# Attention scores with tokens on the partitions: exponentials with row sums, shares turned by DMA, and a listed step order, in a fused attention and gated feed-forward kernel

## The chip, the cores and the metric

The kernel runs on one NeuronCore of a Trainium2 chip. The metric is the device time of one execution in microseconds (us); lower is better. The time before is 1031.74 us, the median of 3 runs (1031.52 to 1032.04).

A core has five engines that run side by side, each through its own instructions in order, and that wait for one another by semaphores: TensorE (PE, matrix products; PEld is its weight load), VectorE (DVE), ScalarE (ACT), GpSimd (POOL) and SyncE (SP), which here only issues DMAs. SBUF is the working memory of 128 partitions; PSUM is the memory of eight banks that TensorE writes to (a bank holds 512 fp32 for each partition).

## The reference

Four images, each with 12288 tokens and a map that is pooled to 768 keys; the keys are also the values. Softmax attention is followed by a gated feed-forward layer.

```python
B, C, Hh, Ww = (4, 128, 384, 32)            # q: (4, 12288, 128), kv: (4, 384, 32, 128)
kv_pool = kv.reshape(B, H // r, r, W // r, r, C).mean(axis=(2, 4))    # r = 4
kv_flat = kv_pool.reshape(B, -1, C) @ w_sr
k = v = kv_flat                             # 768 keys of 128
s = scale * (q @ k.transpose(0, 2, 1))
s = s - s.max(-1, keepdims=True)
a = np.exp(s)
a /= a.sum(-1, keepdims=True) + 1e-09
x = (a @ v).reshape(B * S, D)               # 49152 tokens of 128
gate = np.maximum(x @ w_gate, 0.0)          # 128 x 1536
val = x @ w_val                             # 128 x 1536
out = gate * val @ w_out                    # 1536 x 128
```

## The kernel before

The tokens are worked through in 96 tiles of T = 512, 24 for each image. The 768 keys are six chunks of 128 (`NJC`), the 1536 inner features twelve blocks of 128 (`NFB`). The first four tiles' attention and some of the feed-forward layer are in an opening of its own, a list of words (`OPENING`, lines 69 to 79). From then on a loop over k (line 610) runs over the tiles, and within it a loop over twelve steps (line 621). Each k works on several tiles at once: the scores of tile k, the values of tile k-1, the feed-forward projections of tile k-3 (`LAG` = 3), the output projection of tile k-4. The order of the program is the order on each engine (`manual_schedule`): no scheduler moves anything.

One step issues:

- `out_proj` (line 398): one matmul of 512 columns into the tile's output bank.
- `value_proj` (line 372): one matmul of 512 columns; ScalarE copies it as fp16 to `val` (line 378).
- on even steps `scores` (line 290): one chunk of 128 keys is stationary and the 512 tokens move, so keys lie on the partitions of the bank; ScalarE's exponential (line 295) writes fp16 to `aT`.
- on odd steps `values` (line 297), twice: `aT` is stationary, 128 tokens at a time, and the values of one chunk move, 128 columns and a column of ones that gives the sum of the exponentials. 24 such matmuls make a tile. When half of the tokens are done, VectorE takes the reciprocal of the sums (`keep_sums`, line 313) and multiplies (`keep_values`, line 321) into `x16`; after the second half a DMA transpose of four blocks of 128x128 (`x_turn`, line 329) turns `x16` to `xT`, with features on the partitions, as the projections need it.
- `gate_proj` (line 381): one matmul of 512 columns, then VectorE's `hT = max(gate, 0) * val` (line 388).

After the last step VectorE turns the output bank in 32x32 blocks (`out_turn`, line 415), GpSimd scales it (line 423), and in the next tile four stores go out from SP (line 634).

Ahead of each of the images 1 to 3, in the last 12 or so tiles of the image before, the next keys are made: loads of `kv` by SP (line 184), additions of pixels by GpSimd (`pool_pixels`, lines 190 to 202, one run for each of six tiles), a transpose by VectorE and DMAs (`turn_blocks`, line 265), a projection (`project`, line 257), and a DMA transpose to values (line 284). The queries come in groups of four tiles: GpSimd issues the loads (line 114), SP a transpose of 16 blocks (line 124).

All eight PSUM banks are one pool that is handed out in turn (`bank`, line 87). SP issues the DMAs of its queue in the order of the program.

Of the kernel before, what the change touches and what calls it, by code (L numbers as in the profile page):

```python
# [16 lines left out]
def kernel(  # L17
# [41 lines left out]
    LEAD = GRP  # L59
    qk_scale = 1.0 / math.sqrt(C)  # L60
# [18 lines left out]
    """.split()  # L79
    SUMS = [{}, {}, {}, {"a": [0, 1], "b": ["s", 2]}, {"a": [0, 1], "b": ["s", 2], "c": ["s", 3]}, {"a": [0, 1]}]  # L80
# [4 lines left out]
    psum = ctx.enter_context(tc.tile_pool(name="psum", bufs=8, space=bass.MemoryType.PSUM))  # L85

    def bank(shape, dtype=FP32):
        return psum.tile(shape, dtype, tag="bank", name="bank_ps")
# [38 lines left out]
    def q_load_pair(i):  # L127
        q32 = work.tile([128, 2, NS, C], FP32, tag="q32", bufs=2, name="q32")
        nc.sync.dma_start(  # L129
            q32, q[0, i * T : (i + 2) * T, :].rearrange("(p i s) c -> p i s c", i=2, s=NS)  # L130
        )
        for n in range(2):
            q32s[i + n] = q32[:, n]
# [24 lines left out]
    def q_turned(i):  # L158
        copy_on(f"qT{i}", qTs[0][:, i * NS : (i + 1) * NS, :], q_banks.pop(i))
# [16 lines left out]
    def kv_load(b, pair, lines=range(r), queues=(nc.sync,)):  # L176
        if (b, pair) not in kv_in:
            kv_in[b, pair] = work.tile([128, r, 2, r, C], FP32, tag="kv_in", bufs=3, name="kv_in")
# [4 lines left out]
        for dh in lines:  # L183
            queues[dh % len(queues)].dma_start(  # L184
                parts[:, dh].rearrange("p h dw c -> p (h dw c)"), rows[dh]
            )
# [3 lines left out]
    def pool_pixels(eng, b, pair, h):  # L190
        parts = kv_in[b, pair]
        s2 = work.tile([128, 2, r, C], FP32, tag="kv_s2", bufs=1)
        for i in range(2):
            eng.tensor_tensor(s2[:, i], parts[:, 2 * i, h], parts[:, 2 * i + 1, h], op=ALU.add)  # L194
# [9 lines left out]
    def line(chunk, dh):  # L204
        return kv_in[0, chunk // 2][:, dh, chunk % 2]
# [26 lines left out]
    def turned(name, chunk):  # L232
        kvT = work.tile([128, 128], FP32, tag="kvT_chunk", bufs=3, name="kvT_chunk")
        copy_on(name, kvT, kv_Ts[chunk])
# [8 lines left out]
    def keep_keys(name, jc):  # L243
        pr, engine = key_ps.pop(jc), engine_of(name)
# [9 lines left out]
    def keep_chunk_values(name, jc):  # L254
        copy_on(name, kv16[:, 0, jc, C : 2 * C], value_ps.pop(jc))

    def project(b, pair):
        pr = bank([128, 4, 2, 32])
        nc.tensor.matmul(pr, w_sr_f32, kv_Ts.pop((b, pair)), start=True, stop=True)  # L259
        nc.vector.tensor_scalar(  # L260
            kv16[:, b, 2 * pair : 2 * pair + 2, 0:C].rearrange("c h (i p) -> c h i p", p=32),
            pr.rearrange("c i h p -> c h i p"), 1.0 / (r * r), None, op0=ALU.mult,
        )

    def turn_blocks(b, pair):

        blocks = work.tile([128, 4, 2, 32], FP32, tag="kv_blocks", bufs=2)
# [22 lines left out]
    def scores(k, jc):  # L290
        if k not in aTs:
            aTs[k] = work.tile([128, NJC, T], FP16, tag="aT", bufs=5, name="aT")
        s_ps = bank([128, T])
        nc.tensor.matmul(s_ps, kv16[:, k // NST, jc, 0:C], qT_of(k), start=True, stop=True)  # L294
        nc.scalar.activation(aTs[k][:, jc, :], s_ps, AF.Exp, scale=qk_scale)  # L295

    def values(k, jc, half):
        if jc == 0:
            x_banks[k, half] = bank([128, 2, C + 1])
            if half == 0:  # L300
                x16s[k] = work.tile([128, NS, C], FP16, tag="x16", bufs=3, name="x16")
        x_ps = x_banks[k, half]
        for i in range(2):
            s = 2 * half + i
            nc.tensor.matmul(  # L305
                x_ps[:, i, :], aTs[k][:, jc, s * 128 : (s + 1) * 128],
                kv16[:, k // NST, jc, C : 2 * C + 1],
                start=(jc == 0 and i == 0), stop=(jc == NJC - 1), skip_group_check=True,
            )

    def keep_sums(k, half):
        rinvs[k, half] = work.tile([128, 2, 1], FP32, tag="rinv", bufs=4, name="rinv")
        nc.vector.reciprocal(rinvs[k, half], x_banks[k, half][:, :, C : C + 1])  # L313

    def keep_values(k, half, engine=nc.vector):
        x_ps, rinv = x_banks.pop((k, half)), rinvs.pop((k, half))
        if engine is nc.scalar:
            for i in range(2):
                nc.scalar.mul(x16s[k][:, 2 * half + i, :], x_ps[:, i, 0:C], rinv[:, i])
        else:  # L320
            nc.vector.tensor_tensor(  # L321
                x16s[k][:, 2 * half : 2 * half + 2, :], x_ps[:, :, 0:C],
                rinv.to_broadcast([128, 2, C]), op=ALU.mult,
            )

    def x_turn(k):
        x16 = x16s.pop(k)
        xT = work.tile([128, NS, 128], FP16, tag="xT", bufs=5, name="xT")
        nc.sync.dma_start_transpose(xT, x16.rearrange("p s c -> p (s c)"))
        xTs[k] = xT.rearrange("c s p -> c (s p)")  # L330

# [12 lines left out]
    def lead_kept(name, k):  # L344
        xTs[k] = work.tile([128, NS, 128], FP16, tag="xT", bufs=5, name="xT").rearrange("c s p -> c (s p)")
        copy_on(name, xTs[k], x_banks.pop(k))
# [12 lines left out]
    def lead_scales():  # L359
        turned = work.tile([128, NS * 4, 32], FP32, tag="o_sb", bufs=3, name="sums_turned")  # L360
        nc.vector.transpose(turned.rearrange("p x m -> p (x m)"), x_banks.pop("sums"))
# [9 lines left out]

    def value_proj(k, fb):
        va_ps = bank([128, T])
        nc.tensor.matmul(  # L374
            va_ps, wv16[:, fb * 128 : (fb + 1) * 128], xTs[k], start=True, stop=True
        )
        val = work.tile([128, T], FP16, tag="val", bufs=6, name="val")
        nc.scalar.copy(val, va_ps)  # L378
        vals[k, fb] = val

    def gate_proj(k, fb):
        if k not in hTs:
            hTs[k] = work.tile([128, NFB, T], FP16, tag="hT", bufs=3, name="hT")
        g_ps = bank([128, T])
        nc.tensor.matmul(  # L385
# [313 lines left out]
```

## Time and profile before

| | us |
|---|---|
| median of 3 runs | 1031.74 |
| the profiled execution | 1031.77 |
| its span, from the first instruction to the last | 1029.7 |
| from one tile's DMA transpose of `x16` to the next | 10.42 |

The profile is of one execution. Busy time is time in which an engine worked on an instruction; TensorE's matmuls are pipelined, so that one of 512 columns lasts 380 ns while the next one starts 216 ns after it. In the lists of groups each line has: line of the code, engine, operation, what is written and what is read, shapes, count, then the busy time in us, the mean ns of one, and the engine's idle time just ahead of them with what ended it. The answer by stretches of time has, for each stretch: its length, busy us of PE, PEld, DVE, ACT and POOL (with the number of instructions), the granted clock of TensorE as a fraction, the mean busy share of the 16 DMA engines, and GB/s. A timeline has: start in us, length in us, engine (SPq is SP issuing a DMA), line, operation, names and shapes. The DMA issues of a steady stretch show what SP does in a tile:

```profile
498.48 1.22 SPq L329 DMA_TRANSPOSE xT<-x  x1
499.79 2.59 SPq L634 DMA_DIRECT2D out_dram<-o_sb  x4
508.90 1.21 SPq L329 DMA_TRANSPOSE xT<-x  x1
510.30 3.90 SPq L124 DMA_TRANSPOSE qT<-q  x1
514.28 2.60 SPq L634 DMA_DIRECT2D out_dram<-o_sb  x4
519.33 1.21 SPq L329 DMA_TRANSPOSE xT<-x  x1
```

### The profile page before, as it was taken

What the parts mean: (1) busy time and instruction counts of PE and PEld (TensorE: products, weight loads), DVE (VectorE), ACT (ScalarE), POOL (GpSimd) and SP (SyncE); (2) the same over time, 40 slices, a digit from 0 to 9 for tenths busy, and PEclk for the clock granted to TensorE, in tenths of its full rate; (3) what the DMA queues carried; (4) which work ended last, traced back from release to release, by engine and by line L of the source; (5) the groups of instructions that cost most, each with busy time, mean ns of one, the idle gap of its engine ahead of it and who ended that gap; (6) DMA issues with size and microseconds to landing.
All of it is one profiled execution on the core that took longest, in us unless ns stands there. A gap on an engine that the chain in (4) does not pass through costs nothing.

```text
span 1029.7 us, 19928 instructions
## 1 busy us (share of the span) xinstructions
PE 1023.3 (99%) x6521; PEld 541.8 (53%) x6521; DVE 908.1 (88%) x1663; ACT 909.3 (88%) x1745; POOL 284.5 (28%) x308
## 2 busy tenths in 40 slices
PE   8999999999999999999999999999999999999998
PEld 5455555555555555555555555555555555555555
DVE  3889899998989898998889898989898898989898
ACT  5988899888889888888988889988888988888987
POOL 2502156511211124742112121664121221111110
PEclk9999999999999999999999999999999999999999
DMA  9836386352553648826346167573552434613122
GB/s 321 113 53 83 88 192 148 72 95 39 88 62 55 75 122 160 169 55 88 56 63 88 32 86 154 133 168 58 84 75 45 73 54 66 87 32 65 34 42 52
DMA packets 327807, 93.33 MB, mean 91 GB/s; under 512 B 307480, under 2 KB 320664, under 8 KB 327704
## 3 DMA queue, kind: packets, MB, share of 16 engines
q1 hardware_dynamic: 312584, 77.97, 37.8%
q0 software_dynamic: 14688, 12.98, 11.0%
q8 instruction: 51, 0.84, 0.3%
q10 hardware_dynamic: 432, 1.11, 0.3%
q14 instruction: 52, 0.43, 0.1%
HBM read 53.94 MB, written 26.35 MB: 78 GB/s over the span
## 4 chain that ended last, share of the span: by engine, by line
PE 97%; DMA 2%; SPq 0%; issue 0%; ACT 0%; ACTq 0%
PE bank_ps L374 24%; PE bank_ps L385 24%; PE bank_ps L407 23%; PE bank_ps L305 12%; PE bank_ps L294 12%; DMA kv_in<-in_kv_dram 1%; PE bank_ps L393 1%; DMA q<-in_q_dram 1%; PE bank_ps L259 0%; PE bank_ps L339 0%; PE bank_ps L353 0%; SPq L184 0%; PE bank_ps L227 0%; SPq L502 0%; PE bank_ps L241 0%; SPq L129 0%
## 5 line engine op out<-in xcount | busy, mean ns | idle before, releaser
L388 DVE SCALAR_TENSOR_TENSOR hT<-bank_ps,val 128x512 f16<-128x512 f32 x1152 | 757.2, 686 | 91.0 <-ACT val L378 70.6
L378 ACT CAST val<-bank_ps 128x512 f16<-128x512 f32 x1152 | 677.6, 590 | 103.0 <-PE bank_ps L374 100.8
L374 PE MATMUL bank_ps<-xT,wv 128*128 128x512 f16 x1152 | 436.9, 380 | 0.0
L385 PE MATMUL bank_ps<-xT,wg 128*128 128x512 f16 x1152 | 436.6, 379 | 0.0
L407 PE MATMUL bank_ps<-hT,wo 128*128 128x512 f16 x1116 | 423.5, 380 | 0.0
L295 ACT ACTIVATE aT<-bank_ps 128x512 f16<-128x512 f32 x576 | 345.7, 604 | 0.6 <-PE bank_ps L294 0.6
L423 POOL TENSOR_SCALAR o_sb<-o_t 128x512 f32<-128x512 f32 x89 | 132.4, 1487 | 664.8 <-DVE rinv L313 646.8
L305 PEld LDWEIGHTS <-aT 128*128 128x128 f16 x2208 | 170.6, 98 | 130.3
L294 PE MATMUL bank_ps<-qT,kv 128*128 128x512 f16 x576 | 217.5, 379 | 0.0
L305 PE MATMUL bank_ps<-kv,aT 128*128 128x129 f16 x2208 | 215.5, 221 | 0.0
L374 PEld LDWEIGHTS <-wv 128*128 128x128 f16 x1152 | 112.6, 98 | 133.2 <-issue 0.7
L385 PEld LDWEIGHTS <-wg 128*128 128x128 f16 x1152 | 112.7, 98 | 68.2 <-DMA wg<-in_moe_w_gate_dram 0.3
L407 PEld LDWEIGHTS <-wo 128*128 128x128 f16 x1116 | 109.1, 98 | 66.1 <-DMA wo<-in_moe_w_out_dram 0.4
L294 PEld LDWEIGHTS <-kv 128*128 128x128 f16 x576 | 56.3, 98 | 67.1 <-DVE kv L248 0.4
L321 DVE TENSOR_TENSOR x<-bank_ps,rinv 128x256 f16<-128x256 f32 x184 | 78.1, 425 | 6.4
L415 DVE STREAM_TRANSPOSE o_t<-bank_ps 128x512 f32<-128x512 f32 x93 | 65.7, 706 | 0.0
L114 POOL DMA_DIRECT2D q<-in_q_dram x84 | 46.0, 553 | 0.3 <-ACT val L378 0.3
L194 POOL TENSOR_TENSOR s<-kv_in 128x512 f32<-128x512 f32 x36 | 44.8, 1265 | 0.0
L313 DVE RECIPROCAL rinv<-bank_ps 128x2 f32<-128x2 f32 x184 | 26.8, 146 | 0.0
L196 POOL TENSOR_TENSOR s<-s 128x512 f32<-128x512 f32 x18 | 22.8, 1265 | 1.4
L198 POOL TENSOR_TENSOR c<-s 128x256 f32<-128x256 f32 x18 | 13.0, 725 | 1.4
L393 PEld LDWEIGHTS <-hT 128*128 128x128 f16 x144 | 10.1, 98 | 5.8
(66 smaller groups left out, 121.1 us busy)
## 6 DMA issues: line engine op xcount, KB each, us to landing
kv_in<-in_kv_dram SPq DMA_DIRECT2D x46, 512.0 KB, 7.3
out_dram<-o_sb SPq DMA_DIRECT2D x353, 64.0 KB, 2.2
q<-in_q_dram POOLq DMA_DIRECT2D x84, 128.0 KB, 4.7
xT<-x SPq DMA_TRANSPOSE x92, 2.4
out_dram<-o_sb SPq DMA_DIRECT2D x80, 16.0 KB, 1.5
placed<-blocks SPq DMA_DIRECT2D x9, 128.0 KB, 1.9
kvT<-placed SPq DMA_DIRECT2D x36, 32.0 KB, 1.9
kv_in<-in_kv_dram ACTq DMA_DIRECT2D x2, 512.0 KB, 7.2
```

The lines of the kernel that those rows point to most:

```text
L114: nc.gpsimd.dma_start(q16[32 * j : 32 * (j + 1)].rearrange("t (i s) c -> t i s c", i=GRP), rows[j])
L294: nc.tensor.matmul(s_ps, kv16[:, k // NST, jc, 0:C], qT_of(k), start=True, stop=True)
L295: nc.scalar.activation(aTs[k][:, jc, :], s_ps, AF.Exp, scale=qk_scale)
L305: nc.tensor.matmul(x_ps[:, i, :], aTs[k][:, jc, s * 128 : (s + 1) * 128], kv16[:, k // NST, jc, C : 2 * C + 1], start=(jc == 0 and i == 0) ...
L321: nc.vector.tensor_tensor(x16s[k][:, 2 * half : 2 * half + 2, :], x_ps[:, :, 0:C], rinv.to_broadcast([128, 2, C]), op=ALU.mult,)
L374: nc.tensor.matmul(va_ps, wv16[:, fb * 128 : (fb + 1) * 128], xTs[k], start=True, stop=True)
L378: nc.scalar.copy(val, va_ps)
L385: nc.tensor.matmul(g_ps, wg16[:, fb * 128 : (fb + 1) * 128], xTs[k], start=True, stop=True)
L388: nc.vector.scalar_tensor_tensor(hTs[k][:, fb, :], g_ps, 0.0, vals.pop((k, fb)), op0=ALU.max, op1=ALU.mult)
L407: nc.tensor.matmul(o_banks[k], wo16[:, fb, :], hTs[k][:, fb, :], start=fb == 0, stop=fb == NFB - 1)
L415: nc.vector.transpose(o_t, o_banks.pop(k))
L423: nc.gpsimd.tensor_scalar(to, o_by, 1.0 / X_SCALE**2, None, op0=ALU.mult)
```

## The change

From the fifth tile on (those of the loop) the scores are made with the tokens on the partitions. `score_block` (the word s) takes 128 tokens as stationary and moves all 768 keys, as 512 and 256 columns, into a tile of two banks, of which there is one. `exp_block` (e) is one exponential of 768 elements, which also writes the sum of each token's exponentials. A tile later `invert` (r) takes the reciprocals of the sums, `share` (n) multiplies the fp16 exponentials in place by reciprocal and scale, and each of the four blocks is turned by a DMA transpose of six 128x128 blocks (`a_turn`). Another tile later `values` (x) has the values stationary and the 512 tokens moving, six matmuls, and the result is `xT` at once: `keep_values` (kA) is a plain copy by VectorE, and `keep_sums`, `x16` and `x_turn` are gone.

PSUM is now six single banks, taken from a list in the order in which the program frees them, and the tile of two banks; the opening has all eight until its last eight words. Products and what drains them are now issued apart (v and y, g and h, `project` and `keep_projected`), in the order of a list `STEADY`, the same for each tile. Two of the four stores of an output move from SP to GpSimd. The loads of the next image go out one line at a time, three steps apart, into two buffers instead of three; a few buffers of the opening share memory with later ones.

```diff
+    LAST = [f"{head}{n}" for n in range(NFB) for head in "ovygh"] + ["oT"]
+    STEADY = """
+        s0 g6 o0 e0 v6 y6 v10 r o1 v9 tb s1 y10 h6 o2 n3 g7 o3 v7 o4 y9 v8 v1 y7 o5 o6
+        g1 n0 g9 y1 o7 e1 n1 n2 o8 h7 v0 g10 o9 h9 o10 y0 y8 v3 h1 v2 h10 o11 y3 oT s2
+        g0 h0 e2 g2 g8 h8 x0 y2 h2 x2 v11 x5 s3 g11 x4 y11 x3 v5 e3 x1 y5 h11 v4 y4 P g4
+        kA pk g5 h5 g3 h4 h3
+    """.split()
...
     def bank(shape, dtype=FP32):
-        return psum.tile(shape, dtype, tag="bank", name="bank_ps")
+        n = next(n for n in free_banks if n < usable[0])
+        free_banks.remove(n)
+        ps = pools[n // 6].tile(shape, dtype, tag=f"bank{n}", bufs=1, name="bank_ps")
+        bank_numbers[id(ps)] = n, ps
+        return ps
...
+    def score_block(k, s):
+        b = k // NST
+        if s == 0:
+            a16s[k] = work.tile([128, NS, J], FP16, tag="a16", bufs=4, name="a16")
+            a_sums[k] = work.tile([128, NS], FP32, tag="a_sums", bufs=2, name="a_sums")
+        s_ps = s_banks[s] = wide.tile([128, 1024], FP32, tag="wide", name="wide_ps")
+        qT = qTs[k // GRP][:, k % GRP * NS + s, :]
+        for j0, j1 in ((0, 4), (4, NJC)):
             nc.tensor.matmul(
-                x_ps[:, i, :], aTs[k][:, jc, s * 128 : (s + 1) * 128],
-                kv16[:, k // NST, jc, C : 2 * C + 1],
-                start=(jc == 0 and i == 0), stop=(jc == NJC - 1), skip_group_check=True,
+                s_ps[:, j0 * 128 : j1 * 128], qT, kv16[:, b, j0:j1, 0:C], start=True, stop=True
             )
...
+    def exp_block(k, s):
+        nc.scalar.activation(
+            a16s[k][:, s, :], s_banks.pop(s)[:, 0:J], AF.Exp, scale=qk_scale, accum_out=a_sums[k][:, s : s + 1]
+        )
+
+    def invert(k):
+        inverse = work.tile([128, NS], FP32, tag="inverse", bufs=2, name="inverse")
+        nc.vector.reciprocal(inverse, a_sums[k])
+        a_sums[k] = inverse
+        aTs[k] = work.tile([128, NJC, T], FP16, tag="aT", bufs=AT_BUFS, name="aT")
+
+    def share(k, s):
+        nc.vector.tensor_scalar(
+            a16s[k][:, s, :], a16s[k][:, s, :], a_sums[k][:, s : s + 1], X_SCALE,
+            op0=ALU.mult, op1=ALU.mult,
+        )
+
+    def a_turn(k, s0, s1):
+        aT = aTs[k].rearrange("k j t -> k (j t)").rearrange("k (x p) -> k x p", p=128)
+        nc.sync.dma_start_transpose(
+            aT[:, s0 * NJC : s1 * NJC], a16s[k][:, s0:s1, :].rearrange("p s j -> p (s j)")
+        )
+
+    def values(k, jc):
+        first = k not in x_banks
+        if first:
+            x_banks[k], x_left[k] = bank([128, T]), NJC
+        x_left[k] -= 1
+        aT = aTs[k].rearrange("k j t -> k (j t)").rearrange("k (s j p) -> k j s p", s=NS, j=NJC)
+        nc.tensor.matmul(
+            x_banks[k], kv16[:, k // NST, jc, C : 2 * C], aT[:, jc],
+            start=first, stop=x_left[k] == 0,
+        )
+
+    def keep_values(k):
+        xT = work.tile([128, NS, 128], FP16, tag="xT", bufs=4, name="xT")
         xTs[k] = xT.rearrange("c s p -> c (s p)")
+        nc.vector.tensor_copy(xTs[k], freed(x_banks.pop(k)))
...
+    for at, word in enumerate(OPENING):
+        usable[0] = 8 if at < len(OPENING) - 8 else 6
         open_step(word)
...
+    opening.close()
+    wide = ctx.enter_context(tc.tile_pool(name="psum_wide", bufs=1, space=bass.MemoryType.PSUM))
...
+    def image_step(k, b, at, step):
+        if step % 3 == 1 and 0 <= at < NJC and at % 2 == 0:
+            kv_load(b, at // 2, [step // 3])
+        if step == 3 and 0 <= at - 2 < NJC:
+            pool_pixels(nc.gpsimd, b, (at - 2) // 2, at % 2)
+        pair, odd = divmod(at - 4, 2)
+        if 0 <= pair < NJC // 2:
+            if moves and step > 4:
+                nc.sync.dma_start(*moves.pop())
...
+        kO, kF, kV = k - LAG - 1, k - LAG, k - 2
+        for word in STEADY if k < last else LAST:
+            head, n = word.rstrip("0123456789"), int(word.lstrip("abcdefghijklmnopqrstuvwxyzADPT") or 0)
+            if head == "o":
+                out_proj(kO, n)
+                for queue in (nc.gpsimd, nc.sync):
+                    if out_moves and n >= 2:
+                        queue.dma_start(*out_moves.pop())
+                if b < B:
+                    image_step(k, b, at, n)
...
+            elif head in ("v", "y", "g", "h"):
+                if kF < NT:
+                    {"v": value_proj, "y": keep_value, "g": gate_proj, "h": gated}[head](kF, n)
+            elif head in ("s", "e"):
+                if k < NT:
+                    {"s": score_block, "e": exp_block}[head](k, n)
+            elif head in ("r", "n"):
+                if LEAD <= k - 1 < NT:
+                    if head == "r":
+                        invert(k - 1)
+                    else:
+                        share(k - 1, n)
+                        a_turn(k - 1, n, n + 1)
...
+            elif LEAD <= kV < NT:
+                if head == "x":
+                    values(kV, n)
+                else:
+                    keep_values(kV)
```

The words o, v, g are the matmuls of the output, value and gate projections, y and h what drains v and g, oT the turning of the outputs, tb, P and pk the steps of the next image's keys.

## The prediction

> **What bounds the kernel now.** I read the busy shares first, then the same shares by stage, the chain of waits, the groups of instructions and last the timeline of one tile. The busy shares alone name three candidates (TensorE 99%, VectorE and ScalarE 88%). The stages decide: TensorE is busy through every microsecond of three long stretches.
>
> ```profile
> PE 1023.3 (99%) x6521; PEld 541.8 (53%) x6521; DVE 908.1 (88%) x1663; ACT 909.3 (88%) x1745; POOL 284.5 (28%) x308
> ```
>
> ```profile
> 60.00:340.00 280.00, 280.00 (x1771) 147.25 (x1769) 251.66 (x460) 250.97 (x482) 80.15 (x80) 1.00 0.49 87
> 340.00:620.00 280.00, 280.00 (x1771) 147.26 (x1770) 251.91 (x463) 251.08 (x482) 84.57 (x85) 1.00 0.54 91
> 620.00:900.00 280.00, 280.00 (x1774) 147.43 (x1773) 251.85 (x461) 251.11 (x482) 82.99 (x82) 1.00 0.51 91
> ```
>
> The chain that ended last is TensorE too, and the answer to the chain query gives each line's share to a tenth:
>
> ```profile
> by line: PE bank_ps L374 24.2%; PE bank_ps L385 24.1%; PE bank_ps L407 23.4%; PE bank_ps L305 12.2%; PE bank_ps L294 11.8%; DMA kv_in<-in_kv_dram 1.1%; PE bank_ps L393 0.8%; DMA q<-in_q_dram 0.8%; PE bank_ps L259 0.4%; PE bank_ps L339 0.3%;
> ```
>
> So a saving on TensorE counts in full, as long as the other engines still deliver inside a tile. A tile is 10.42 us (the tokens' transposes start at 498.48, 508.90, 519.33). VectorE is busy 251.7 of 280 us, 9.37 us of a tile: it has only 1 us to give. The groups that the change touches, then 1.6 us of VectorE's and GpSimd's timelines:
>
> ```profile
> L388 DVE SCALAR_TENSOR_TENSOR hT<-bank_ps,val 128x512 f16<-128x512 f32 x1152 | 757.2, 686 | 91.0 <-ACT val L378 70.6
> L378 ACT CAST val<-bank_ps 128x512 f16<-128x512 f32 x1152 | 677.6, 590 | 103.0 <-PE bank_ps L374 100.8
> L295 ACT ACTIVATE aT<-bank_ps 128x512 f16<-128x512 f32 x576 | 345.7, 604 | 0.6 <-PE bank_ps L294 0.6
> L423 POOL TENSOR_SCALAR o_sb<-o_t 128x512 f32<-128x512 f32 x89 | 132.4, 1487 | 664.8 <-DVE rinv L313 646.8
> L305 PE MATMUL bank_ps<-kv,aT 128*128 128x129 f16 x2208 | 215.5, 221 | 0.0
> L321 DVE TENSOR_TENSOR x<-bank_ps,rinv 128x256 f16<-128x256 f32 x184 | 78.1, 425 | 6.4
> L415 DVE STREAM_TRANSPOSE o_t<-bank_ps 128x512 f32<-128x512 f32 x93 | 65.7, 706 | 0.0
> ```
>
> ```profile
> 655.81 2.49 POOL L194 TENSOR_TENSOR s<-kv_in 128x512 f32<-128x512 f32 x2
> 658.38 1.27 POOL L196 TENSOR_TENSOR s<-s 128x512 f32<-128x512 f32 x1
> 659.73 0.72 POOL L198 TENSOR_TENSOR c<-s 128x256 f32<-128x256 f32 x1
> 660.53 0.45 POOL L202 TENSOR_TENSOR kv_s<-c 128x128 f32<-128x128 f32 x1
> ```
>
> In the groups, the mean of one is its latency; back to back the engines overlap. Four L388 at 508.75 take 2.47 us, 0.617 each; ScalarE starts at 499.44, 499.92 and 500.41, so 0.49 each. In the last fence, GpSimd pools the next image's pixels in one run of 5.2 us. That happens in 18 tiles (L194 x36, two for each), six ahead of each new image.
>
> **What the Trainium skill says.** "VectorE: DVE Perf Modes", the perf-mode tier table: a tensor_scalar on 16-bit data in SBUF runs at four elements a cycle, 693 ns for 2048. The trace has no such row; its nearest, the opening's 128x512 casts from SBUF at L98 (422 ns, against 692 from PSUM), does show an SBUF source going faster. "SBUF — State Buffer", Who interferes with whom: such an instruction takes a port pair that VectorE shares with GpSimd; the pair is an exclusive lock, and whoever comes second "fully blocks" until the first instruction ends. No run here shows it: the steady VectorE work of before reads PSUM. "ScalarE: Activation LUTs", What ACT_TABLE_LOAD costs: 186 ns + 0.833 ns an element; for 512 that is 613 ns, and the trace has 604.
>
> **The change part by part.** *TensorE.* From the chain, L305 costs 0.122 x 1029.7 / 2208 = 0.0569 us, and the 512-column lines (L374, L385, L407) 738 us / 3420 = 0.216. Values go from 24 x 0.0569 = 1.366 to 6 x 0.216 = 1.295 us a tile. Scores go from six of 512 columns to four pairs of 512 + 256; the slope between 129 and 512 columns gives 0.109 for 256, so 1.300 against 1.296. Net -0.066 us a tile, x 92 tiles = -6.0 us. Tile ideal: 10.36. Moving the values one tile later moves no TensorE work out of the loop.
>
> *ScalarE.* Six exponentials x 0.49 become four of 768. By the page one is 826 ns, less the 0.10 overlap that the trace shows (590 against 490), plus the sum it now writes out, which no row shows: nothing to 0.2 us (the opening's one-column activation is 203 ns); I take 0.08, so 0.80. Sum: 12 x 0.49 + 4 x 0.80 = 9.1 us of 10.36; hidden. The tightest run is e2 y2 y11 e3 y5, whose end frees the bank of g3: it starts 6.8 us into the tile, and g3 goes at 10.14, so it holds up to about 0.87 us an exponential. At 0.95 it costs 0.15 us a tile, 14 us in all.
>
> *VectorE.* Out: two L321 and two L313. In: four shares, a copy of the values (like L388, 0.617) and one reciprocal (0.13). A share, estimated from the page's 693 ns: 160 ns fixed + 768/4/0.96 = 360 ns, less the overlap of 0.07 (686 against 617): 0.29. Sum: 12 x 0.617 + 0.63 (L415, by the start of what follows it) + 0.617 + 4 x 0.29 + 0.13 = 9.94 us, 96% of a tile. At half the rate a share is 0.49 and the sum 10.74, at a quarter 0.89 and 12.3: then VectorE is the bound.
>
> *The listed order.* I laid the list out on TensorE at 0.216 a matmul (0.325 for a score block), a result being readable 0.42 us after its matmul's start (500.76 to ScalarE's start at 501.18). Shares come to run from 2.6 to 4.0 us after the tile's start, the turning of the outputs ends at 7.1, the values' copy runs 9.7 to 10.4, and g6 of the next tile, which needs it, goes at 10.69. Each of the six banks' releases comes ahead of its next matmul; the closest are h4 for v9 and y5 for g3 (under 0.1 us). VectorE keeps 0.4 us idle. So plain tiles fit: loss taken as nothing, with up to 0.1 us x 74 = 7 us for the thin margins. One two-bank score tile holds each score block until its exponential is done: e0 ends near 1.33 and s1 goes at 1.62.
>
> *GpSimd against the shares.* In a plain tile GpSimd scales the outputs from 7.1 to 8.6 and then issues two stores: the shares at 2.6 meet nothing. In the 18 pooling tiles its run of 5.2 us starts after the stores, near 10.0, and lasts to 4.8 us of the next tile, right across the shares. The first share waits for the second-level add (2.2 to 3.5): 0.9 us. If VectorE then keeps the port, that is all; if they alternate, 0.7 and 0.45 us follow, so 0.9 to 1.9, and nothing if the lock doesn't bind. I take 1.4 less 0.3 of idle time, which is less than 0.4 because the image's own transposes and copies (0.43 and 0.42, L268 and L260) fall on it too. Queued behind a share are h7 (whose bank g10 wants at 4.96, with its release then due at 5.7), h9 and h1, so TensorE waits for all of it: 18 x 1.1 = +20 us. The release point moves with the tile, so it repeats.
>
> *SP, DMA.* Four a-turns of six blocks replace one of four, and SP hands two of four stores to GpSimd. A turn holds SP 1.21 us for one block or four and at least 1.92 for 16 (3.83 in the middle, beside loads), so 1.33 to 1.65 for six. Per tile 5.3 to 6.6, stores 1.3, a quarter of a q turn 1.0, gaps 0.7: 8.3 to 9.6 of 10.36. On the rings four blocks took 0.64 us of all 16 engines (share 0.85 over 499.65 to 500.40), so 24 take 3.8. The values read them at 7.2 us of the following tile, some 7 us after the last lands. In six tiles per image SP also issues about 15 us of loads and moves, which leaves it 3 to 10 us behind: hidden, or up to 3 us late per image. Taken as nothing.
>
> *Opening and end.* The last eight opening words have six banks: up to 1 us. Ends: nothing.
>
> Sum against the profiled execution (span 1029.7, 1031.77 with what lies around it; the median is 1031.74, so the same): 1031.8 - 6.0 + 20 = 1046 us.
>
> **The rivals.**
> *A, TensorE stays the bound (24%).* The shares and GpSimd don't disturb each other, or idle time takes it up, and the thin margins hold. For it: the 0.4 us of VectorE, a walk in which every release is in time. Against: 96% on an in-order engine. It gives 1031.8 - 6.0 = 1026; it turns slower than before once stalls pass 0.065 us a tile.
> *B, an engine overfull in every tile (22%).* The shares run at half rate (10.74 + 0.4 of waits against 10.36) or the exponentials with sums cost 0.95 and more: +0.15 to +0.8 us x 92, so 1040 to 1100, middle 1065. At a quarter rate, which the page speaks against (3% of it), 1200.
> *C, turned shares late (12%).* SP at 1.65 us a turn plus the image's moves: 3 us late, three times, beside part of the port's cost: 1030 to 1045.
> That the change doesn't do what it says is not a rival: the order of the program has four shares in a row after h6 and six 512-column values.
>
> **How the numbers follow.** Forecast 42%, with its own range 1035 to 1062 (18 x 0.5 to 1.8 us, plus 0 to 4). A 24%, B 22%, C 12%. The range 1026 to 1085 leaves out the slower part of B and the very best of A. What can be told from no change is about 0.2%, 2 us: A gives most of faster (0.24) and some of same; C's lower end the rest of same (0.06); slower 0.70.
>
> **What would show it.** Right: gaps on TensorE only around pooling tiles, shares there of 1 us and more against 0.36 in plain ones, plain tiles at 10.36. B: idle TensorE in every tile, a share near 0.56 us or an exponential above 0.95. C: values' weight loads waiting for DMA. Wrong: TensorE busy throughout at 10.36, or shares of one length in all tiles.

## The result and the profile after

The changed kernel takes 1076.02 us (median of 4 runs, 1072.16 to 1079.41) against 1031.87 for the kernel before on the same chip: a ratio of 1.0427, interval 1.0381 to 1.0474. It is slower by 44 us; the forecast was 14. The profiled execution took 1079.16 us; its span is 1077.4, which is 47.7 more than before.

The page of the changed kernel, busy shares and the groups that answer to those shown of before (L451 drains the gate projection, L439 the value projection, L378 is the values, L361 the shares, L350 the exponentials):

```profile
PE 1035.4 (96%) x5049; PEld 490.9 (46%) x5049; DVE 1006.0 (93%) x1847; ACT 936.0 (87%) x1929; POOL 424.7 (39%) x524
...
L451 DVE SCALAR_TENSOR_TENSOR hT<-bank_ps,val 128x512 f16<-128x512 f32 x1152 | 725.5, 678 | 27.6 <-PE bank_ps L443 21.3
L439 ACT CAST val<-bank_ps 128x512 f16<-128x512 f32 x1152 | 621.5, 590 | 80.0 <-PE bank_ps L432 50.6
...
L378 PE MATMUL bank_ps<-aT,kv 128*128 128x512 f16 x552 | 182.1, 385 | 15.0 <-DMA kvT<-placed 7.4
...
L361 DVE TENSOR_SCALAR a<-a,inverse 128x768 f16<-128x768 f16 x368 | 155.3, 484 | 0.0
...
L350 ACT ACTIVATION_READ_ACCUMULATOR a<-wide_ps 128x1 f32 x368 | 72.6, 197 | 0.0
```

TensorE has less work than before in the loop and yet 12 us more of busy time (1035.4 against 1023.3): something makes it slower while it works. The stretches of time for the same three windows as before (columns: length, busy us of PE, PEld, DVE, ACT and POOL, granted clock, DMA share, GB/s):

```profile
60.00:340.00 280.00, 268.65 (x1267) 125.24 (x1266) 266.26 (x488) 244.22 (x504) 118.94 (x143) 0.98 0.85 144
340.00:620.00 280.00, 267.83 (x1278) 125.56 (x1277) 267.26 (x488) 246.27 (x510) 114.77 (x131) 0.99 0.84 145
620.00:900.00 280.00, 268.53 (x1277) 125.59 (x1275) 267.41 (x489) 245.84 (x508) 116.71 (x136) 0.99 0.89 147
```

TensorE, which before was busy in every microsecond of these stretches, now idles 11.4, 12.2 and 11.5 us of 280; the granted clock is under 1; the DMA engines' mean share went from about 0.5 to between 0.84 and 0.89. The chain of work that ended last agrees, with VectorE and two DMAs in it (the answer breaks off at its end):

```profile
by line: PE bank_ps L443 19.0%; PE bank_ps L432 18.8%; PE bank_ps L471 18.0%; PE bank_ps L378 10.1%; PE wide_ps L345 9.5%; DVE hT L451 6.1%; DVE a L361 4.5%; DMA aT<-a 4.1%; DMA kvT<-placed 2.0%; issue 1.2%; DMA kv_line<-in_kv_dram 1.1%; DV
```

What TensorE waited for (line, releaser: us in total, times, longest):

```profile
PE bank_ps L443 <- DVE hT L451: 19.9, 13, 2.6
PE bank_ps L378 <- DMA kvT<-placed: 7.4, 3, 2.8
PE bank_ps L378 <- DMA aT<-a: 7.3, 4, 3.0
```

There are two waits: 19.9 us for banks that VectorE drains late, and 14.7 us for turned shares. (The name kvT<-placed in the middle line is the release that came last by the profile; a move of the next image's sums is no input of L378. In each of those three cases a turn of shares landed 0.25 us before L378 started.) Nearly all stalls are in tiles that prepare an image. From one turning of the outputs (L479) to the next, in the ten tiles that prepare the second of the loop's images, in us:

```
tile (0, 2, 4: kv lines; 2 to 7: pixel sums; 1, 5, 9: q turn and q load)
 0      1      2      3      4      5      6      7      8      9
10.36  13.55  11.76  11.94  13.13  12.62  11.68  10.72  10.37  13.83
```

A row's entry k is the time from L479 of tile k to that of tile k + 1. Over all three images these tiles hold 52.0 us beyond 10.36 each. Outside them two tiles of the loop lose 0.8 us together and the others nothing, as VectorE's timeline near the end shows:

```profile
1024.75 1.40 DVE L361 TENSOR_SCALAR a<-a,inverse 128x768 f16<-128x768 f16 x4
...
1028.74 0.72 DVE L479 STREAM_TRANSPOSE o_t<-bank_ps 128x512 f32<-128x512 f32 x1
...
1035.12 1.40 DVE L361 TENSOR_SCALAR a<-a,inverse 128x768 f16<-128x768 f16 x4
...
1039.11 0.72 DVE L479 STREAM_TRANSPOSE o_t<-bank_ps 128x512 f32<-128x512 f32 x1
```

L479 to L479 is 10.37 us here, and the four shares take 1.40 us. Now a tile with pixel sums, in the first of the loop's images, VectorE's timeline first, then GpSimd's:

```profile
151.35 0.72 DVE L479 STREAM_TRANSPOSE o_t<-bank_ps 128x512 f32<-128x512 f32 x1
...
157.73 4.35 DVE L361 TENSOR_SCALAR a<-a,inverse 128x768 f16<-128x768 f16 x4
162.00 2.47 DVE L451 SCALAR_TENSOR_TENSOR hT<-bank_ps,val 128x512 f16<-128x512 f32 x4
164.43 0.72 DVE L479 STREAM_TRANSPOSE o_t<-bank_ps 128x512 f32<-128x512 f32 x1
```

```profile
156.67 2.50 POOL L223 TENSOR_TENSOR s<-kv_in 128x512 f32<-128x512 f32 x2
159.25 1.28 POOL L225 TENSOR_TENSOR s<-s 128x512 f32<-128x512 f32 x1
160.60 0.72 POOL L227 TENSOR_TENSOR c<-s 128x256 f32<-128x256 f32 x1
161.40 0.46 POOL L231 TENSOR_TENSOR kv_s<-c 128x128 f32<-128x128 f32 x1
```

The same four shares take 4.35 us, 2.95 more, and the tile 13.08. One at a time, they last 1.67, 1.42, 0.88 and 0.61 us, and the last ends 0.2 us after GpSimd's last addition: as long as GpSimd has additions, each share lasts until one of them is over. The Trainium skill ("SBUF — State Buffer", Who interferes with whom) says that VectorE and GpSimd share a port pair that is an exclusive lock; the trace now agrees. In 16 tiles the four shares took over 1.6 us, 26.4 us longer than 1.40 in all.

The other wait, from the DMA issues of SP in the first loop image, and the stretches of time around it:

```profile
125.05 0.62 SPq L213 DMA_DIRECT2D kv_in<-in_kv_dram  x1
125.76 1.24 SPq L368 DMA_TRANSPOSE aT<-a  x1
127.05 0.59 SPq L213 DMA_DIRECT2D kv_in<-in_kv_dram  x1
127.74 2.71 SPq L368 DMA_TRANSPOSE aT<-a  x2
130.50 0.58 SPq L213 DMA_DIRECT2D kv_in<-in_kv_dram  x1
131.26 10.77 SPq L144 DMA_TRANSPOSE qT<-q  x1
```

```profile
120.00:130.00 10.00, 10.00 (x50) 4.69 (x48) 9.76 (x20) 9.30 (x20) 2.73 (x4) 1.00 0.79 184
130.00:135.00 5.00, 5.00 (x26) 2.35 (x25) 4.97 (x12) 4.48 (x10) 2.43 (x5) 1.00 1.19 180
135.00:140.00 5.00, 2.86 (x14) 1.17 (x12) 4.36 (x8) 3.45 (x8) 1.91 (x2) 1.00 1.28 161
140.00:145.00 5.00, 5.00 (x16) 2.02 (x17) 1.51 (x3) 2.55 (x5) 4.76 (x6) 0.66 1.20 234
145.00:150.00 5.00, 5.00 (x26) 2.34 (x24) 5.00 (x12) 4.36 (x11) 1.14 (x2) 1.00 0.76 137
```

In front of and among a tile's turns of shares (L368) stand three 512-KB lines of the next image (L213), and behind them a turn of q that holds SP for 10.77 us; at most 5.1 in the kernel before. The DMA share, which adds up the times of packets that can overlap, goes over 1 from 130 us on, and TensorE is idle for 2.14 us between 135 and 140 until turned shares land. A turn lands 2.8 us after its issue at the median, and 10.9 at worst. In the fourth line the clock is 0.66: after the stall TensorE runs slower for a while, though it isn't idle at all.

So of the 47.7 us between the two spans the trace places 43.2: −6.0 on the plain tile, +19.9 waiting for drained banks, +14.7 for turned shares, +10.2 for the clock (six falls from 60 to 900 us, each of 3.41 us at half the clock), +4.4 at the ends (below). Of the rest about 3.3 is an estimate: a matmul's record outlasts the next one's start by 0.16 us (380 less 216 ns), so each of the 20 stalls reads that much short. This says where the time shows, not yet what each cause would give back.

### The profile page after: what moved, and what is told of

Its sections match the earlier page's. It is cut to its first block, busy times and chain, and to the rows that moved or that the text cites. A ratio compares the mean times of both kernels' runs of the same rounds, so it can differ in the third digit from the quotient of the medians.

```text
span 1077.4 us, 17334 instructions
## 1 busy us (share of the span) xinstructions
PE 1035.4 (96%) x5049; PEld 490.9 (46%) x5049; DVE 1006.0 (93%) x1847; ACT 936.0 (87%) x1929; POOL 424.7 (39%) x524
## 4 chain that ended last, share of the span: by engine, by line
PE 77%; DVE 12%; DMA 8%; issue 1%; SPq 0%; ACT 0%; DVEq 0%; ACTq 0%
PE bank_ps L443 19%; PE bank_ps L432 19%; PE bank_ps L471 18%; PE bank_ps L378 10%; PE wide_ps L345 9%; DVE hT L451 6%; DVE a L361 5%; DMA aT<-a 4%; DMA kvT<-placed 2%; DMA kv_line<-in_kv_dram 1%; DVE xT L386 1%; DMA q<-in_q_dram 1%; PE bank_ps L457 1%; ACT a L350 0%; DMA kv_in<-in_kv_dram 0%
## 5 line engine op out<-in xcount | busy, mean ns | idle before, releaser
L451 DVE SCALAR_TENSOR_TENSOR hT<-bank_ps,val 128x512 f16<-128x512 f32 x1152 | 725.5, 678 | 27.6 <-PE bank_ps L443 21.3
L439 ACT CAST val<-bank_ps 128x512 f16<-128x512 f32 x1152 | 621.5, 590 | 80.0 <-PE bank_ps L432 50.6
L443 PE MATMUL bank_ps<-xT,wg 128*128 128x512 f16 x1152 | 362.0, 381 | 20.4 <-DVE hT L451 19.9
L350 ACT ACTIVATE a<-wide_ps 128x768 f16<-128x768 f32 x368 | 299.2, 813 | 43.6 <-PE wide_ps L345 38.2
L378 PE MATMUL bank_ps<-aT,kv 128*128 128x512 f16 x552 | 182.1, 385 | 15.0 <-DMA kvT<-placed 7.4
L345 PE MATMUL wide_ps<-kv,qT 128*128 128x512 f16 x736 | 181.6, 329 | 0.3
L361 DVE TENSOR_SCALAR a<-a,inverse 128x768 f16<-128x768 f16 x368 | 155.3, 484 | 0.0
L710 POOL DMA_DIRECT2D out_dram<-o_sb x216 | 138.4, 651 | 27.9 <-POOL o_sb L487 20.5
L345 PEld LDWEIGHTS <-qT 128*128 128x128 f16 x736 | 72.5, 99 | 90.2 <-issue 5.2
L378 PEld LDWEIGHTS <-kv 128*128 128x128 f16 x552 | 54.1, 99 | 74.2 <-issue 19.5
L479 DVE STREAM_TRANSPOSE o_t<-bank_ps 128x512 f32<-128x512 f32 x93 | 66.4, 714 | 11.4 <-PE bank_ps L471 2.2
L350 ACT ACTIVATION_READ_ACCUMULATOR a<-wide_ps 128x1 f32 x368 | 72.6, 197 | 0.0
L386 DVE CAST xT<-bank_ps 128x512 f16<-128x512 f32 x92 | 63.6, 691 | 7.3 <-PE bank_ps L378 0.7
```

Source lines behind the costliest of these rows:

```text
L345: nc.tensor.matmul(s_ps[:, j0 * 128 : j1 * 128], qT, kv16[:, b, j0:j1, 0:C], start=True, stop=True)
L350: nc.scalar.activation(a16s[k][:, s, :], s_banks.pop(s)[:, 0:J], AF.Exp, scale=qk_scale, accum_out=a_sums[k][:, s : s + 1])
L361: nc.vector.tensor_scalar(a16s[k][:, s, :], a16s[k][:, s, :], a_sums[k][:, s : s + 1], X_SCALE, op0=ALU.mult, op1=ALU.mult,)
L378: nc.tensor.matmul(x_banks[k], kv16[:, k // NST, jc, C : 2 * C], aT[:, jc], start=first, stop=x_left[k] == 0,)
L386: nc.vector.tensor_copy(xTs[k], freed(x_banks.pop(k)))
L439: nc.scalar.copy(vals[k, fb], freed(proj_banks.pop(("v", k, fb))))
```

## The experiments

Two theories. The port: shares wait for GpSimd's pixel sums. The DMA: shares are turned late, since SP's queue and the DMA rings carry too much when an image is prepared. The rival to both is that the listed order or the exponential loses time in every tile, which the 10.37 above already speaks against. All kernels ran beside the kernel before, whose median lay between 1031.6 and 1032.1.

| kernel | median us | ratio to before, interval |
|---|---|---|
| 1: no images prepared in the loop | 1026.08 | 0.9944 (0.9929 to 0.9959) |
| 2: no pixel sums | 1063.17 | 1.0304 (1.0263 to 1.0345) |
| 3: sums after the shares | 1063.35 | 1.0312 (1.0295 to 1.0329) |
| 4: no kv loads in the loop | 1067.21 | 1.0347 (1.0330 to 1.0364) |
| 5: new order in SP's queue | 1063.12 | 1.0305 (1.0290 to 1.0320) |
| 6: new order, sums after | 1056.38 | 1.0237 (1.0222 to 1.0252) |
| 7: new order, sums after, spread loads | 1036.73 | 1.0050 (1.0035 to 1.0066) |
| 8: new order, spread loads | 1059.00 | 1.0257 (1.0230 to 1.0284) |
| 9: as 7, q loaded late | 1037.74 | 1.0049 (1.0035 to 1.0063) |
| 10: sums after, spread loads | 1051.36 | 1.0172 (1.0142 to 1.0203) |
| 11: as 9, q work in pieces | 1040.33 | 1.0081 (1.0067 to 1.0095) |
| 12: sums after, q turn late | 1059.37 | 1.0275 (1.0233 to 1.0318) |
| 13: as 6, moves ahead of loads | 1049.35 | 1.0159 (1.0132 to 1.0186) |

### What the kernel is without the images

```diff
-        b = k // NST + 1
+        b = B
         at = k % NST - (NST - NJC - 6)
...
-    x_banks[k], kv16[:, k // NST, jc, C : 2 * C], aT[:, jc],
+    x_banks[k], kv16[:, 0, jc, C : 2 * C], aT[:, jc],
```

(the scores' b likewise)

> Leaves out the making of the keys of images 1 to 3 (loads, pixel sums, moves, projection); all tiles use image 0's keys. Both theories (shares that wait for GpSimd; turned shares that come late) put all of the loss in the tiles that make keys, so every tile of the loop should take 10.36 us and the time should be 1079.2 - 53 = 1026 us (1024 to 1029). If the listed order itself were overfull, tiles would stay above 10.36 here.

Measured: 1026.08, as forecast for a loop that loses nothing. The new way of making scores, shares and values, with its listed order, loses nothing by itself; what the loop loses comes with the images. It also sizes the ends: its span is 1024.2, while before's 1029.7 less 6.0 and less the 3.9 us that before pays for the keys' products is 1019.8. So 4.4 us lie outside the steady tiles; that they lie at the head (about 1.4) and in the drain (about 2.7) is read from the traces, not tried.

### Taking one cause away

No pixel sums: GpSimd copies 128 elements in place of five additions.

```diff
-        for i in range(2):
-            eng.tensor_tensor(s2[:, i], parts[2 * i][:, h], parts[2 * i + 1][:, h], op=ALU.add)
...
+        eng.tensor_copy(
+            s3s[b, pair][:, :, h], kv_in[b, pair][3][:, h, 0].rearrange("p (j c) -> p j c", c=32)
+        )
```

> Leaves out the pixel sums of images 1 to 3: GpSimd copies 128 elements of one line in place of five additions; loads, moves and projections stay. Shares wait for GpSimd: the 18 pooling tiles lose their 32 us but for the moves' own, so about 1046 us, shares of 0.35 us in every tile, while the tiles at 1 and 9 keep their 20 us. Turned shares late as the cause of all: 1070 us or more.

Sums after the shares: the same additions, held by a copy that reads what h7 wrote, which stands behind the last share on VectorE.

```diff
-        if step == 3 and 0 <= at - 2 < NJC:
-            pool_pixels(nc.gpsimd, b, (at - 2) // 2, at % 2)
...
+                if head == "h" and n == 7 and b < B and 0 <= at - 2 < NJC:
+                    nc.gpsimd.tensor_copy(gate, hTs[kF][:, 7, 0:1])
+                    pool_pixels(nc.gpsimd, b, (at - 2) // 2, at % 2)
```

> The pixel sums stay whole, but GpSimd waits for the gated product h7, which comes right after the four shares, before it starts them. Shares wait for GpSimd: as good as without the sums, about 1046 us, shares of 0.35 us in every tile. If it were GpSimd's work itself (its time, or its reads of SBUF), and not its place against the shares: no change from 1076.

No kv loads in the loop: images 1 to 3 pool image 0's rows again.

```diff
+        if b > 0:
+            kv_in[b, pair] = kv_in[0, pair % 2]
+            return
```

> Leaves out the loads of images 1 to 3; GpSimd sums image 0's rows again, in the same places. Turned shares late behind the loads: the tiles at 1 lose their 9 us, the pooling tiles part of theirs, 1060 to 1067 us. Shares wait for GpSimd: the shares of the pooling tiles stay as long as they are (1 us and more), so not under 1050.

Measured: 1063.17, 1063.35 and 1067.21. The first two expectations, near 1046, failed, and by the same 17 us; the third number fits what either theory had forecast for it. With the sums held, each share is short again (481 ns at most), but TensorE now waits 20.9 us for turned shares, where it had waited 14.7:

```profile
PE bank_ps L378 <- DMA aT<-a: 13.6, 9, 2.9
PE bank_ps L378 <- DMA kvT<-placed: 7.3, 3, 3.9
```

Without the loads it is the other way round. The waits for turned shares fall to 1.9 us, and those for drained banks grow from 19.9 (the gate projection is L446 in that kernel):

```profile
PE bank_ps L446 <- DVE hT L454: 25.8, 17, 2.6
```

So the two causes cover for each other: undoing one brings forth more of the other, and neither difference from the changed kernel is the price of what was undone. A reading that fits, though no run separates it, is that while the shares hold VectorE up every tile is longer, and the DMA catches up in that time.

### SP's order, the loads' places and the sums' start, in combination

The new order: in a tile, SP issues the turn of q, the moves, the value turns (their hunk is left out below) and the kv lines behind the last turn of shares.

```diff
-        if step % 3 == 1 and 0 <= at < NJC and at % 2 == 0:
-            kv_load(b, at // 2, [step // 3])
+        if step >= 8 and 0 <= at < NJC and at % 2 == 0:
+            kv_load(b, at // 2, [step - 8])
...
-            if moves and step > 4:
+            if moves and step > 7:
...
-            q_turn(g + 1)
             q_load(g + 2)
...
+                if n == 8 and ph == 1:
+                    q_turn(g + 1)
```

> The turn of q (issued once in four tiles), the moves of the transposed sums, the turns of the image's values and the kv loads are issued by SP behind the last turn of shares of their tile instead of ahead of it; their number and bytes are the same, and the pixel sums still start where they did. If the turned shares are late because they stand behind other issues in SP's queue, the stalls of the tiles with a q turn go, but the shares still wait for GpSimd: about 1063. If they are late because the DMA rings carry too much, the order is worth nothing: 1073 to 1077.

> The same order in SP's queue, and the pixel sums held until the shares of the tile are done (which alone gave 1063). If the queue's order makes the shares late, both causes are gone: 1032 to 1040. If the traffic makes them late: 1056 to 1063.

Spread loads: the twelve kv lines of an image go out over eleven tiles instead of three, at the tenth output step; the pixel sums stand in tiles that don't load q, and the moves, turns and products of the keys come every fourth tile (part of the edit):

```diff
+    LINES = {
+        -8: [(0, 0)], -7: [(0, 1)], -6: [(0, 2)], -5: [(0, 3)], -4: [(1, 0)], -2: [(1, 1)],
+        -1: [(1, 2)], 0: [(1, 3)], 2: [(2, 0)], 3: [(2, 1), (2, 2)], 4: [(2, 3)],
+    }
...
+        if step == 9:
+            for pair, dh in LINES.get(at, []):
+                kv_load(b, pair, [dh])
```

> As the kernel with the order and held sums, and the twelve kv loads of an image go out one a tile over eleven tiles instead of four in each of three tiles, with the pixel sums in tiles that load no q. If traffic was what was left, 1030 to 1034 (1026 without the images, and 4 for the three keys' products on TensorE); if the order alone decided, the same as that kernel.

> Loads spread and the queue's order changed, the pixel sums started where they were (the third output step), two tiles in four, none of which loads q. Only the shares' wait for GpSimd is left: at 1.7 us in each of 18 tiles, 1030 + 31 = about 1060; if the wait cost only through what it did to the queue, 1030 to 1036.

> As the kernel with loads spread, order and held sums, but with SP's order as in the changed kernel: the turn of q at the head of its tile, the moves from the fifth output step, the turns of the image's values at the second. If the order matters by itself, each of 22 tiles with a q turn loses 1 to 2 us as in the held sums' kernel: 1045 to 1055. If it mattered only because the loads were in the way: 1036 to 1039.

Measured: with the new order alone 1063.12, as forecast if only the shares' wait is left. What TensorE waits for there is the drained banks; no turned share is late any more:

```profile
PE bank_ps L443 <- DVE hT L451: 25.5, 17, 2.6
```

Held sums and the new order came to 1056.38, not to the 1032 to 1040 of a queue whose order is all; with the loads spread as well to 1036.73, some 3 us above the range given. With both loads and order mended, the sums' start decides between 1059.00 and 1036.73. VectorE's shares, one line of the answer for L361 in each (after the count: shortest, median and longest in ns), first with the sums where they were, then after the shares:

```profile
L361 DVE TENSOR_SCALAR a<-a,inverse x368: 401/416/1761, 49.8 to 1027.9; 128x768 f16<-128x768 f16 x184
```

```profile
L361 DVE TENSOR_SCALAR a<-a,inverse x368: 400/416/463, 49.5 to 1003.0; 128x768 f16<-128x768 f16 x184
```

One edit apart, 22.3 us: this is the shares' wait for GpSimd by itself, with nothing to cover it. Tiles with sums take 11.67 to 13.35 us there and plain ones 10.36, so 1.3 more at the least. That 1059.00 lies so near the 1060 expected is luck: the wait had been put at 31 us, and what is left without it at 1030. And with the sums held in both, the DMA by itself is 1063.35 less 1036.73, 26.6 us. Together they gave 39.3, so some 10 of the 49 overlap.

Of the DMA's part neither half is enough: held sums with spread loads give 1051.36 (in the range given if the order matters by itself; a tile's one line stands behind the turns of shares there too), with the new order alone 1056.38, with both 1036.73. In the stretches of the kernel with both, TensorE is busy throughout two of the three windows, at a DMA share of 0.80 to 0.88, nearly that of the changed kernel:

```profile
60.00:340.00 280.00, 276.67 (x1325) 130.14 (x1324) 268.70 (x508) 255.05 (x527) 121.88 (x151) 0.99 0.86 156
340.00:620.00 280.00, 280.00 (x1351) 132.36 (x1350) 273.81 (x518) 259.71 (x539) 127.30 (x153) 1.00 0.88 157
620.00:900.00 280.00, 280.00 (x1352) 132.54 (x1351) 273.92 (x518) 259.89 (x539) 113.91 (x135) 1.00 0.80 143
```

So it isn't the mean of the traffic, the same 153.5 MB, but its bunching and its order in SP's queue. In this kernel a turn of q holds SP 3.8 us at most, and a turn of shares lands after 8.4 at most.

### What the order alone left

With the new order and held sums, TensorE's list had changed:

```profile
PE wide_ps L288 <- DMA kvT<-placed: 14.3, 3, 5.8
PE bank_ps L378 <- DMA aT<-a: 3.4, 3, 1.6
```

The values are nearly in time, and now the keys' product (L288) waits for the moves, which my own order had put one at a time between that tile's 512-KB lines. Two runs took this apart. In the first, of the new order only the turn of q is moved; in the second, which is kernel 6 with the edit below, all four moves go ahead of the lines:

```diff
-            if moves and step > 7:
-                nc.sync.dma_start(*moves.pop())
+            if step == 8:
+                while moves:
+                    nc.sync.dma_start(*moves.pop())
```

> The kernel with the sums held until the shares are done (1063.4), and of SP's order only the turn of q is moved, from the head of its tile to behind the tile's turns of shares; moves and loads stay. If the q turn ahead of the shares' turns is the main cause of their lateness, the values' waits (20.9 us in that kernel) mostly go: 1040 to 1048. If moves and loads between the turns do it: 1055 to 1063.

> The kernel with the new order and held sums (1056.4), with the four moves of the transposed sums all issued at the ninth output step and ahead of that tile's kv loads, instead of one at a step between them. If its stalls (14.3 us of TensorE waiting at the keys' product for the moves) come from the moves standing among 512-KB loads: 1036 to 1042. If the bunched loads make the turned shares late as well: 1050 to 1056.

Measured: 1059.37, so the turn of q explains only about 4 us of 26.6, within the runs' own spread (1055.67 to 1066.47), and this theory fell; the number lies in the range given if moves and loads between the turns do it. The second gave 1049.35 (1045.93 to 1057.68), just under the range given if bunched loads make the shares late too. In its profile, which is of its slowest execution, 1057.68, the wait at the product is gone, and the turned shares are late again:

```profile
PE bank_ps L378 <- DMA aT<-a: 18.6, 9, 4.4
```

This shows where the stall went, not what the other executions gained. As far as these two show, the lateness goes to whatever stands behind the bunched lines. The Trainium skill ("DMA: Bandwidth & Descriptors", Queues, rings and completion order) says that SP has one row of rings, consumed in order on each DMA engine; turns, moves and lines all being SP's, that fits. That another queue for the lines would help was not tried.

### What remains

The best of these, 1036.73, is 10.7 above the kernel without images. Of that, 4.1 are nine keys' products of 0.46 us each (tiles of 10.82), and 4.8 are one tile of 15.2 us, from 94.8 us on, while the first of the loop's images is prepared, where the DMA share is 1.23 between 90 and 100 us. Two kernels were to take that tile away. First, GpSimd loads q at the tile's end, and one line goes out two tiles later:

```diff
-        if ph == 1:
-            q_load(g + 2)
...
+                if n == 11 and ph == 1:
+                    q_load(g + 2)
```

> As the kernel with loads spread, order and held sums (1036.7), and GpSimd issues the load of q at the tile's last output step instead of at its head, and the first image's fifth line is loaded two tiles later, so that the stretch at 85 to 110 us, where the rings were full and one tile took 15.2 us, carries less. If that stretch is the rest, its 4.8 us go: 1031.5 to 1033 (1026.1 without the images, 4.1 for nine products on TensorE, and about 1 for a tile of 11.3). If not: 1036 to 1037.

Second, the same with the q turn in four pieces and the q load over three tiles (part of the edit):

```diff
+                    nc.sync.dma_start_transpose(
+                        qTs[g1][:, at4], q16s[g1][:, at4].rearrange("p s c -> p (s c)")
+                    )
+                if n == 11 and ph > 0:
+                    q_load(g + 2, [[0], [1], [2, 3]][ph - 1])
```

> As the kernel with the late load of q (1037.7), and the turn of q goes out as four pieces, one a tile, and the load of q over three tiles, so that no tile carries more than one of each; bytes are the same. If what is left (three to five tiles of 11 to 14 us) is the burst of a q turn, a q load and a kv line in one tile: 1031 to 1034, at best 1030.3 (1026.1 without the images, and nine products of 0.46). If the rings are overfull on the mean in the image stretches: 1036 to 1039, with stalls in other tiles.

Measured: 1037.74 (1033.78 to 1039.35) and 1040.33; both missed, and both lie above even the range given for the case that the theory is wrong. The 15.2 became 13.7, then 11.5, and other tiles grew: to 12.2 and 12.3 in the first, to between 11.2 and 13.2 in five tiles of the second, where GpSimd also waits 42.5 us for turns of q before it can load into their buffers. So what is left is not one burst of q's; which transfers collide in it stays open. No version beats the kernel before. The floor by these numbers, 1026.1 + 4.1 = 1030.2, is 1.6 us below it.

## Why the prediction was wrong in its size

*TensorE, −0.066 us a tile, plain tile 10.36*: right. Plain tiles are 10.36 to 10.37. That the kernel without images came at the very 1026 of rival A is luck: it does without 3.9 us of keys' products, and pays 4.4 at the ends.

*ScalarE, an exponential at 0.80*: right. ScalarE's timeline:

```profile
1028.99 0.81 ACT L350 ACTIVATE a<-wide_ps 128x768 f16<-128x768 f32 x1
1029.70 0.19 ACT L350 ACTIVATION_READ_ACCUMULATOR a<-wide_ps 128x1 f32 x1
1029.79 1.08 ACT L439 CAST val<-bank_ps 128x512 f16<-128x512 f32 x2
```

From one exponential to the next instruction 0.80 us. The sum comes out by an instruction of its own of 194 ns, which overlaps the exponential's end by 0.11.

*VectorE, a share at 0.29 by the page's figure*: too low. It is 0.35 back to back (1.40 for four), and 413 ns alone against the estimate of 360. By the same sum VectorE is then busy for 10.18 of 10.36 us, and plain tiles still fit, so it cost nothing there.

*The listed order, no loss*: right, by the same tiles. Rival B is out.

*GpSimd against the shares, 1.1 net in 18 tiles, +20*: right in mechanism, and near in size. TensorE's wait at the very line named, the gate projection, is 19.9 us; alone the cause costs 22.3. The prediction's 1.4 of delay in each tile was 1.5 on the mean (26.4 over 18), though uneven, from nothing to 3.1. That they alternate is what happened.

*SP and DMA, "taken as nothing"*: the step that failed. Its plain tile was not too cheap: a turn of shares holds SP 1.24 us at the median, less than the 1.33 to 1.65 priced. What failed is the conclusion for the image's tiles, "hidden, or up to 3 us late per image", which set SP's backlog against 7 us of slack and priced each issue as in a plain tile, without what the rings carry at that moment. Where kv lines and a q load were under way, the DMA share passed 1, a turn of q held SP for up to 10.8 us, not 3.83, and a turn of shares landed after up to 10.9 us, against 2.8 at the median. Alone this costs 26.6 us, three times the 9 us that rival C had at most; beside the port still 17 (1076.0 less 1059.0).

*TensorE's clock*: not in the sum at all. The stalls cost some 10 us a second time, by a lower clock after them; this is a part of both causes' prices.

*Opening and end, at most 1 and nothing*: 4.4 us. The values come one tile later, so the drain may hold one more step; no run shows that this is why.

The forecast had its sign from the one cause that it priced; the other cause, taken as nothing, is as large.

## What to carry to other kernels

When a change moves work into DMA transposes, price the queue in its busiest stretch and not in a plain one: add up, tile by tile, what SP issues and the share that it takes of the rings, and what stands ahead of the transfer that TensorE needs next. Spread bulk loads, and put them behind the small urgent transfers: here either alone gave 7 to 12 us, and both 26.6. And when two causes share a tile, undo both and then each alone: a single undoing showed 13 and 17 us for causes worth 22 and 27.

## What was not expected of the hardware

The granted clock fell after short stalls: of the nine stalls of 1.9 us and more in the changed kernel's image stretches, six, of 2.15 to 2.59 us, were followed by 4 us at a clock of 0.57 to 0.65; after the other three, of 1.93, 2.84 and 3.01 us, it stayed 1.00. The Trainium skill ("TensorE: Matmul & The Clock Gate", What's actually happening) gives an idle window of about 3.4 us for it; here less was enough, and it isn't the length of the stall alone that decides. The clock records of the trace show what does. The six falls start whole numbers of 3.413 us apart, and each lasts 3.41 us. Counted in steps of that length (the ends of matmuls are modelled in these records), TensorE had been idle for 2.13 to 2.35 us of the step before each fall, and no step with 1.93 us or less of idle time was followed by one. The stalls of 2.84 and 3.01 us each lay across two steps, with at most 1.8 us in either. The other kernels have 22 more falls from the full clock, all after at least 2.08 us, and none after 1.94 or less.

GpSimd's additions don't slow VectorE where it reads a bank. Of the 1152 gate products drained from PSUM (L451), some beside the same additions, the longest took 693 ns in the changed kernel, with a median of 680.
